# Attention with the last 64 keys of four heads in quarters of the array, two pairs to a turn, and SBUF tiles moved by 32 bytes

## The chip, the cores and the metric

The kernel runs on one core of one Trainium2 chip. The metric is the device time of one execution in microseconds (us). The core has a matrix engine (PE, with its weight loads listed apart as PEld), a vector engine (DVE), a scalar engine (ACT), a general engine (POOL) and a queue engine that issues most DMAs (SP). Operands lie in SBUF, 128 partitions wide; matmul results go to PSUM, which has eight banks of 512 float32 columns per partition.

## What is computed

Three stages follow each other, on 4 batches of 448 tokens, with 12 heads of 64 channels (768 in all):

```python
# 1 attention, per batch and head; q, k, v: (4, 12, 448, 64)
scores = q @ k.T / sqrt(64) - log(448)
x = sigmoid(scores) @ v                      # no softmax: keys can be summed in any order
# 2 gated MLP: w_in 768x1024, w_spatial 448x448, w_out 512x768
h = relu(x @ w_in); u, v = h[..., :512], h[..., 512:]
v_n = (v - mean(v)) / sqrt(var(v) + 1e-6)
v_s = w_spatial @ v_n + b_spatial            # over the tokens of a batch
x = (u * v_s) @ w_out
# 3 MLP with a residual: w_ch1 768x3072, w_ch2 3072x768
xn = (x - mean(x)) / sqrt(var(x) + 1e-6) * g_ln
out = x + relu(xn @ w_ch1) @ w_ch2
```

## The kernel before

**Precision.** Most products are made from operands split in two `float32r` parts, `hi` and `lo`: `mm3` (L258) issues three matmuls, hi x hi (L259), hi x lo (L260) and lo x hi (L261). The product of the attention weights with v is made in plain float32 instead; one such call shows as two rows of PE in the trace, one for each of two passes.

**Memory.** SBUF holds four large tiles that the program cuts up itself: `r_base` and `f_base` for the whole kernel, `r_att` and `f_att` during attention, and after it `r_mlp` and `f_mlp` in their place. The `r_` tiles hold the float32r parts that matmuls read. A tile is placed behind the one before it, rounded up to 32 bytes. `r_base` starts at byte 16,512 of a partition, which is 258 x 64. Behind it the constants (`f_base`, `warm`, the small vectors up to `mhalf`) and the small pool take an odd number of 32-byte steps, so that `r_att`, `f_att`, `r_mlp` and `f_mlp` start 32 bytes past a multiple of 64. All blocks inside a tile are whole multiples of 64 bytes. So an operand is at a multiple of 64 bytes exactly when it lies in `r_base` or `f_base`.

**PSUM.** Two pools: `ps_s` with 2 buffers of two banks (`ps2()`, `wide()`) and `ps_1` with 4 buffers of one bank (`ps1()`). `ps2` takes the scores of a chunk of keys for both heads of a pair, and later the 768 columns of `Project.step` and `ch2`. `ps1` takes the sums of `av`, and the groups of `hv`, `hu`, `spatial`, `ch1` and the transposes of `Project.turn`.

**Attention** (main loop, L755 to L778). The 48 heads are handled as 24 pairs, head `j` of a pair in partitions 64j to 64j+63 of q and k. The host pads k from 448 to 512 keys by repeating the last 64, and the rows of v for the repeated keys are zero. So a pair has four chunks of 128 keys. `qk(p, t)` (L396) does chunks 2t and 2t+1: 6 matmuls of 448 columns each (three products, two heads, each on 64 rows of the array), then one `Sigmoid` on ACT (L410) over 2 x 448 columns. `av(p, t)` (L413) adds up v x weights over the four chunks, head j in columns 64j to 64j+63 of the array (L422). `x_end` (L426) splits a pair's sums into x hi (ACT copy, L288) and x lo (DVE, L289). `qk_split` (L382) makes the parts of q and k for the next pair: casts on DVE (L389, L392), subtractions on POOL (L393, L394) from pair 2 on. The loop runs over half pairs i: `qk(p, 0)`, the split and the loads for later pairs, `av` of the pair before and its `x_end`; then `qk(p, 1)`, and a stretch of background work.

**Background.** `bg` (L743) is a stream of matmul groups of stage 2 for batches 0 to 2: `hv` and `hu`, x times the two halves of w_in, in groups of 18 matmuls. `bg.run(2 * BG_US)` issues some 4.6 us of it, if the x and the weights that it needs are ready (`settled`), else nothing. `jobs.pop` issues weight work: a load on SP, a decode (one ACT op, L277, and three DVE ops, L278 to L282), a split (ACT L288, DVE L289). The four chunks of w_in that `hv` needs come first.

**After attention**: `hv` and `hu` of batch 3, `spatial` (groups of 11 matmuls into `ps1`, each read by one DVE multiply, L558), `Project` (14 steps of 24 matmuls into `wide()`, with `turn`, six transposes, L616, into two `ps1` tiles that ACT and DVE read, L288 and L289), then `mlp`: for each of 12 groups of weights and 4 units of tokens, two groups `ch1` (18 matmuls into `ps1`, read by ACT, L653, then DVE, L654) and the tiles of `ch2` (12 matmuls into `wide()`, read by DVE, L671). In its first group of weights two more `turn`s stand between `ch1` groups (L699). Every engine runs its instructions in program order.

Of the kernel before, what the change touches and what calls it, by code (L numbers as in the profile page):

```python
# [16 lines left out]
P = 128  # L17
B, H, S, D = 4, 12, 448, 64
NPAIR = H // 2
SK = 512  # L20
# [32 lines left out]
PLAIN = range(B * H)  # L53

R_BASE, F_BASE = 23040, 7680
R_ATT, F_ATT = 3840, 9792
# [157 lines left out]
def sigmoid_attention_gmlp_mlp(ctx: ExitStack, tc, q, k, v, w_in, w_sp, w_out, g_ln, w1, w2, out):  # L214
# [4 lines left out]
    ps_s = ctx.enter_context(tc.tile_pool(name="ps_s", bufs=2, space=bass.MemoryType.PSUM))  # L219
    ps_1 = ctx.enter_context(tc.tile_pool(name="ps_1", bufs=4, space=bass.MemoryType.PSUM))  # L220
# [24 lines left out]
    nc.vector.memset(mhalf, -0.5)  # L245

# [100 lines left out]
    k_r = [Ring(R, SK, 2, "att") for _ in range(2)]  # L347
    rv = Ring(F, 512, 3, "att")
    rq = Ring(F, S, 3, "att")
    rk = Ring(F, SK, 3, "att")  # L350
    af_r = Ring(F, 2 * S, 6, "att")
# [13 lines left out]
    @on_pairs  # L365
    def qk_load(p, b, hp):

        qr, kr = rq.next().ap(S), rk.next().ap(SK)
        pairs[p] = dict(raw=(qr, kr))
        for j in range(2):  # L370
            rows = slice(D * j, D * j + D)
            eng = nc.scalar if p < 3 and j else nc.sync
            eng.dma_start(kr[rows], k[b, hp, :, j])
            eng.dma_start(qr[rows], q[b, hp, :D, j])
# [6 lines left out]
    @on_pairs  # L381
    def qk_split(p, b, hp):  # L382
        t = pairs[p]
        qr, kr = t["raw"]
        (qh, ql), (kh, kl) = ([r.next().ap(n) for r in rs] for rs, n in ((q_r, S), (k_r, SK)))
        t.update(qh=qh, ql=ql, kh=kh, kl=kl)
        eng = nc.gpsimd if p > 1 else nc.vector
        if p:
            nc.vector.tensor_copy(kh, kr)  # L389
        else:  # L390
            nc.scalar.copy(kh, kr)
        nc.vector.tensor_copy(qh, qr)  # L392
        eng.tensor_sub(kl, kr, kh)  # L393
        eng.tensor_sub(ql, qr, qh)  # L394

    def qk(p, t):  # L396


        a = pairs[p]
        for c in (2 * t, 2 * t + 1):  # L400
            ps = ps2()
            kc = slice(c * P, (c + 1) * P)
            for i, (w, x) in enumerate((("kh", "qh"), ("kl", "qh"), ("kh", "ql"))):
                for j in range(2):
                    rows = slice(D * j, D * j + D)
                    nc.tensor.matmul(  # L406
                        ps[:, j, :S], a[w][rows, kc], a[x][rows], start=(i == 0), stop=(i == 2)
                    )
            af = af_r.next().ap(2, S)
            nc.scalar.activation(af, ps[:, :, :S], AF.Sigmoid, bias=bias_s, scale=1.0 / math.sqrt(D))  # L410
            a["a", c] = af

    def av(p, t):  # L413

        a = pairs[p]
        if t == 0:
            a["ps"] = ps1()
        for c in (2 * t, 2 * t + 1):
            af = a.pop(("a", c))
            for j in range(2):  # L420
                rows = slice(D * j, D * j + D)
                nc.tensor.matmul(  # L422
                    a["ps"][rows, :S], a["v"][:, 4 * j + c], af[:, j], start=(c == 0), stop=(c == 3)
# [326 lines left out]
    pv_load(0)  # L750
    qk_split(0)
    qk_load(2)
    pv_load(1)
    jobs.pop(1)
    for i in range(2 * n_pairs):  # L755
        p, t = divmod(i, 2)
        now[0] = i
        qk(p, t)
        if t == 0:
            qk_split(p + 1)  # L760
            qk_load(p + 3)
        else:
            pv_load(p + 2)
        if t:
            bg.run(2 * BG_US)
        elif p:
            av(p - 1, 0)
            av(p - 1, 1)
            x_end(p - 1)
        jobs.pop(0 if i < FIRST else 2 if i >= MORE else 1)  # L770
        if i == WO_FROM:
            c0, c1, c2, c3 = wo_chunks
            for job in (c0.load, c1.load, idle, c0.decode, c1.decode, c2.load, c3.load):
                jobs.add([job, idle])
    now[0] += 1
    av(n_pairs - 1, 0)
    av(n_pairs - 1, 1)
    x_end(n_pairs - 1)  # L778
# [172 lines left out]
```

## Time and profile before

| | us |
|---|---|
| median of 3 runs | 1093.79 (1092.7 to 1094.69) |
| the profiled execution | 1092.77 |
| its span, first to last instruction | 1090.8 |
| PE busy, by the page | 1082.0 |
| attention with its background, until | 246.8 |
| `hv`, `hu` of batch 3, and `spatial`, until | 314 |
| `Project`, until | 381 |
| `mlp`, until | 1090.8 |

A row of the timeline is an instruction, or some alike in a row (x12): start, time from the first start to the last end, engine, line, operation, output<-inputs, size, how many; in brackets, idle time of the engine before it and what ended that. Matmuls overlap in the pipeline, so what a matmul costs is read from the distance between starts, not from its length. Row names drop buffer numbers: `r_base,r_mlp` says that one operand lies in the one tile and one in the other. The granted clock (PEclk) is the share of full speed that TensorE had in a stretch.

### The profile page before, as it was taken

Reading aid. Unit: us, or ns where it says so; the run is one execution under the profiler, and the core shown is the slowest. Engines: PE = TensorE matmul, PEld = TensorE weight load, DVE = VectorE, ACT = ScalarE, POOL = GpSimd, SP = SyncE. Lnnn points to the kernel's source line nnn. Section 1 sums busy time; section 2 is a strip of 40 time slices with the busy share of each in tenths; the row PEclk is TensorE's granted clock in tenths of the full one; section 3 lists DMA queues with packets and bytes.
Section 4 is the critical chain, followed back from the end, with each engine's and each line's share of the span. In section 5 each row is a group of like instructions: output and inputs, shape, how many; then the busy total and the mean of one; then the engine's idle time right before and its main releaser. Section 6 shows DMA issues by size and latency. Waiting matters only on the chain.

```text
span 1090.8 us, 14034 instructions
## 1 busy us (share of the span) xinstructions
PE 1082.0 (99%) x5860; PEld 877.3 (80%) x5860; DVE 541.8 (50%) x789; ACT 315.9 (29%) x465; POOL 104.0 (10%) x96
## 2 busy tenths in 40 slices
PE   8999999999999999999999999999999999999998
PEld 5466666668988888888888888888888888888887
DVE  4750113206666856363645555564636364555533
ACT  6754445444533422121112121111212121212110
POOL 1232121202214410000000000000000000000000
PEclk9999999999999999999999999999999999999999
DMA  8743245306610112021111111020202011111013
GB/s 243 220 121 99 94 118 162 122 28 224 208 35 11 48 59 87 29 81 36 59 59 58 59 58 58 29 66 22 88 29 87 30 62 55 58 58 58 1 58 145
DMA packets 31951, 87.94 MB, mean 81 GB/s; under 512 B 7568, under 2 KB 12816, under 8 KB 31760
## 3 DMA queue, kind: packets, MB, share of 16 engines
q1 hardware_dynamic: 29808, 78.97, 22.5%
q0 software_dynamic: 1600, 7.34, 2.0%
q8 instruction: 46, 0.75, 0.3%
q10 hardware_dynamic: 480, 0.74, 0.3%
q14 instruction: 17, 0.14, 0.0%
HBM read 74.17 MB, written 12.86 MB: 80 GB/s over the span
## 4 chain that ended last, share of the span: by engine, by line
PE 99%; ACT 1%; issue 0%; DVE 0%
PE ps L259 28%; PE ps L260 28%; PE ps L261 28%; PE ps L422 7%; PE ps L406 6%; PE ps L616 1%; ACT f_att L410 0%; PE ps L748 0%; PE ps L556 0%; PE ps L555 0%; ACT r_base L288 0%; ACT f_base L277 0%; DVE r_base L289 0%; DVE f_mlp L671 0%; DVE warm L232 0%
## 5 line engine op out<-in xcount | busy, mean ns | idle before, releaser
L671 DVE TENSOR_TENSOR f_mlp<-ps,f_mlp 128x768 f32<-128x768 f32 (+1 forms) x157 | 149.5, 952 | 156.2 <-PE ps L261 156.2
L259 PE MATMUL ps<-r_base,r_mlp 128*128 128x512 f32 (+1 forms) x608 | 216.7, 356 | 0.0
L261 PE MATMUL ps<-r_base,r_mlp 128*128 128x512 f32 (+1 forms) x608 | 216.4, 356 | 0.0
L260 PE MATMUL ps<-r_base,r_mlp 128*128 128x512 f32 (+1 forms) x560 | 197.6, 353 | 0.0
L260 PE MATMUL ps<-r_mlp 128*128 128x512 f32 (+1 forms) x496 | 170.0, 343 | 0.0
L653 ACT ACTIVATE r_mlp<-ps 128x512 fp32r<-128x512 f32 (+1 forms) x96 | 52.1, 543 | 398.5 <-PE ps L261 398.5
L261 PE MATMUL ps<-r_mlp 128*128 128x512 f32 (+1 forms) x460 | 155.2, 337 | 0.0
L259 PE MATMUL ps<-r_mlp 128*128 128x512 f32 x448 | 151.1, 337 | 0.0
L259 PE MATMUL ps<-r_base 128*128 128x512 f32 (+2 forms) x372 | 140.0, 376 | 0.0
L261 PE MATMUL ps<-r_base 128*128 128x512 f32 (+2 forms) x372 | 137.7, 370 | 0.0
L654 DVE SCALAR_TENSOR_TENSOR r_mlp<-ps,r_mlp 128x512 fp32r<-128x512 f32 (+1 forms) x96 | 59.7, 622 | 150.8 <-ACT r_mlp L653 150.8
L261 PEld LDWEIGHTS ps<-r_base,r_mlp 128*128 128x128 f32 x608 | 114.6, 189 | 18.1
L260 PE MATMUL ps<-r_base 128*128 128x512 f32 (+2 forms) x348 | 128.3, 369 | 0.0
L259 PEld LDWEIGHTS ps<-r_base,r_mlp 128*128 128x128 f32 x608 | 114.4, 188 | 17.3
L260 PEld LDWEIGHTS ps<-r_base,r_mlp 128*128 128x128 f32 x560 | 105.3, 188 | 15.0
L260 PEld LDWEIGHTS ps<-r_mlp 128*128 128x128 f32 x496 | 93.4, 188 | 13.0
L410 ACT ACTIVATE f_att<-ps,bias_s 128x896 f32<-128x896 f32 x96 | 91.5, 1005 | 39.3 <-PE ps L406 39.0
L261 PEld LDWEIGHTS ps<-r_mlp 128*128 128x128 f32 x460 | 86.6, 188 | 9.9
L259 PEld LDWEIGHTS ps<-r_mlp 128*128 128x128 f32 x448 | 84.4, 188 | 11.0
L289 DVE TENSOR_TENSOR r_base<-ps,r_base 128x448 fp32r<-128x448 f32 (+1 forms) x48 | 27.3, 586 | 126.8 <-ACT r_base L288 126.8
L259 PEld LDWEIGHTS ps<-r_base 128*128 128x128 f32 x372 | 70.0, 188 | 17.0 <-issue 6.5
L422 PE MATMUL ps<-f_att 128*64 128x448 f32 x384 | 79.1, 555 | 0.0
(90 smaller groups left out, 1216.1 us busy)
## 6 DMA issues: line engine op xcount, KB each, us to landing
f_base<-in_w SPq DMA_DIRECT2D x48, 768.0 KB, 4.2
f_att<-in_v SPq DMA_DIRECT2D x24, 256.0 KB, 2.9
f_base<-in_w_in SPq DMA_DIRECT2D x8, 768.0 KB, 5.3
f_att<-in_k SPq DMA_DIRECT2D x45, 128.0 KB, 3.6
f_att<-in_q SPq DMA_DIRECT2D x45, 112.0 KB, 3.3
out_y<-f_mlp SPq DMA_DIRECT2D x12, 384.0 KB, 2.3
vscr<-f_base SPq DMA_DIRECT2D x14, 256.0 KB, 2.0
uscr<-f_base SPq DMA_DIRECT2D x16, 224.0 KB, 1.9
```

The lines of the kernel that those rows point to most:

```text
L259: nc.tensor.matmul(ps, lh, rh, start=first, stop=False)
L260: nc.tensor.matmul(ps, lh, rl, start=False, stop=False)
L261: nc.tensor.matmul(ps, ll, rh, start=False, stop=last)
L289: eng.tensor_sub(lo, x, hi)
L406: nc.tensor.matmul(ps[:, j, :S], a[w][rows, kc], a[x][rows], start=(i == 0), stop=(i == 2))
L410: nc.scalar.activation(af, ps[:, :, :S], AF.Sigmoid, bias=bias_s, scale=1.0 / math.sqrt(D))
L422: nc.tensor.matmul(a["ps"][rows, :S], a["v"][:, 4 * j + c], af[:, j], start=(c == 0), stop=(c == 3))
L616: nc.tensor.transpose(ps[:, i], xn[:, kc * P : (kc + 1) * P], ident)
L653: nc.scalar.activation(hh[:, f], ps[:, :n], AF.Relu)
L654: nc.vector.scalar_tensor_tensor(hl[:, f], ps[:, :n], 0.0, hh[:, f], op0=ALU.max, op1=ALU.subtract)
L671: nc.vector.tensor_add(y[:, ws], ps, y[:, ws])
```

## The change

- A tile `pad` of 8 float32 (32 bytes) follows `mhalf`, so that the attention tiles and the MLP tiles start at multiples of 64 bytes, as `r_base` does.
- PSUM is cut otherwise: `ps_s` has 3 buffers of two banks, `ps_1` has 2 of one bank. This holds for the whole kernel.
- Attention runs in turns of two pairs. Three chunks of 128 keys are done as before, into three `ps2` tiles. The last 64 keys of the four heads of two pairs are done in one call, `qk_rest`: four plain float32 matmuls on the raw q and k, head j in rows 64j and pair i in columns 64i of the array, then one `Sigmoid`. `av_rest` starts the sums of the two pairs from these, again with four matmuls on 64 rows and 64 columns, into the two banks of one `ps2` tile, and `av` adds the three chunks to it. `sums` does this for the two pairs of the turn before, with both `x_end`s at its end.
- `PLAIN` is empty, so the repeated rows of v are kept (pair i reads rows 64i); k is loaded with 448 columns, not 512. The rings for raw q, k, v and for the weights are deeper.
- In a turn the order is `qk_rest`, `sums`, weight jobs, `qk` of the first pair, a split, loads, weight jobs, background, `qk` of the second pair, a split, loads, weight jobs, background.

```diff
--- before.py
+++ after.py
@@ -17,7 +17,7 @@
 P = 128
 B, H, S, D = 4, 12, 448, 64
 NPAIR = H // 2
-SK = 512
+SM = 3 * P
 DM = H * D
 KC = DM // P
 DFF = 1024
@@ -50,10 +50,11 @@
 VN_DVE = [range(4), range(4), (1, 3), (1, 3)]
 HU_EVERY = 3
 
-PLAIN = range(B * H)
+PLAIN = ()
 
 R_BASE, F_BASE = 23040, 7680
-R_ATT, F_ATT = 3840, 9792
+PAD = 8
+R_ATT, F_ATT = 3328, 12800
 R_MLP, F_MLP = 11904, 9984
 
 PIECE = 1536
@@ -216,8 +217,8 @@
     const = ctx.enter_context(tc.tile_pool(name="const", bufs=1))
     small = ctx.enter_context(tc.tile_pool(name="small", bufs=4))
     dram = ctx.enter_context(tc.tile_pool(name="dram", bufs=1, space=bass.MemoryType.DRAM))
-    ps_s = ctx.enter_context(tc.tile_pool(name="ps_s", bufs=2, space=bass.MemoryType.PSUM))
-    ps_1 = ctx.enter_context(tc.tile_pool(name="ps_1", bufs=4, space=bass.MemoryType.PSUM))
+    ps_s = ctx.enter_context(tc.tile_pool(name="ps_s", bufs=3, space=bass.MemoryType.PSUM))
+    ps_1 = ctx.enter_context(tc.tile_pool(name="ps_1", bufs=2, space=bass.MemoryType.PSUM))
 
     R, F = Arena("r"), Arena("f")
     r_base = const.tile([P, R_BASE], F32R, name="r_base")
@@ -243,6 +244,7 @@
     vnorm = const.tile([P, 2, B, 4], F32, name="vnorm")
     mhalf = const.tile([P, 2, 4], F32, name="mhalf")
     nc.vector.memset(mhalf, -0.5)
+    const.tile([P, PAD], F32, name="pad")
 
     ctx.enter_context(tc.manual_schedule())
 
@@ -344,11 +346,11 @@
     R.add("att", r_att)
     F.add("att", f_att)
     q_r = [Ring(R, S, 2, "att") for _ in range(2)]
-    k_r = [Ring(R, SK, 2, "att") for _ in range(2)]
-    rv = Ring(F, 512, 3, "att")
-    rq = Ring(F, S, 3, "att")
-    rk = Ring(F, SK, 3, "att")
-    af_r = Ring(F, 2 * S, 6, "att")
+    k_r = [Ring(R, SM, 2, "att") for _ in range(2)]
+    rv = Ring(F, 512, 4, "att")
+    rq = Ring(F, S, 4, "att")
+    rk = Ring(F, S, 4, "att")
+    af_r = Ring(F, 2 * S, 8, "att")
     a_rings = [*q_r, *k_r, rv, rq, rk, af_r]
 
     n_pairs = B * NPAIR
@@ -365,12 +367,12 @@
     @on_pairs
     def qk_load(p, b, hp):
 
-        qr, kr = rq.next().ap(S), rk.next().ap(SK)
+        qr, kr = rq.next().ap(S), rk.next().ap(S)
         pairs[p] = dict(raw=(qr, kr))
         for j in range(2):
             rows = slice(D * j, D * j + D)
             eng = nc.scalar if p < 3 and j else nc.sync
-            eng.dma_start(kr[rows], k[b, hp, :, j])
+            eng.dma_start(kr[rows], k[b, hp, :, j, :S])
             eng.dma_start(qr[rows], q[b, hp, :D, j])
 
     @on_pairs
@@ -382,22 +384,28 @@
     def qk_split(p, b, hp):
         t = pairs[p]
         qr, kr = t["raw"]
-        (qh, ql), (kh, kl) = ([r.next().ap(n) for r in rs] for rs, n in ((q_r, S), (k_r, SK)))
+        (qh, ql), (kh, kl) = ([r.next().ap(n) for r in rs] for rs, n in ((q_r, S), (k_r, SM)))
         t.update(qh=qh, ql=ql, kh=kh, kl=kl)
         eng = nc.gpsimd if p > 1 else nc.vector
         if p:
-            nc.vector.tensor_copy(kh, kr)
+            nc.vector.tensor_copy(kh, kr[:, :SM])
         else:
-            nc.scalar.copy(kh, kr)
+            nc.scalar.copy(kh, kr[:, :SM])
         nc.vector.tensor_copy(qh, qr)
-        eng.tensor_sub(kl, kr, kh)
+        eng.tensor_sub(kl, kr[:, :SM], kh)
         eng.tensor_sub(ql, qr, qh)
 
-    def qk(p, t):
+    def sigmoid(ps):
+        af = af_r.next().ap(2, S)
+        nc.scalar.activation(af, ps[:, :, :S], AF.Sigmoid, bias=bias_s, scale=1.0 / math.sqrt(D))
+        return af
+
+    def qk(p):
 
 
         a = pairs[p]
-        for c in (2 * t, 2 * t + 1):
+        a["a"] = []
+        for c in range(3):
             ps = ps2()
             kc = slice(c * P, (c + 1) * P)
             for i, (w, x) in enumerate((("kh", "qh"), ("kl", "qh"), ("kh", "ql"))):
@@ -406,21 +414,39 @@
                     nc.tensor.matmul(
                         ps[:, j, :S], a[w][rows, kc], a[x][rows], start=(i == 0), stop=(i == 2)
                     )
-            af = af_r.next().ap(2, S)
-            nc.scalar.activation(af, ps[:, :, :S], AF.Sigmoid, bias=bias_s, scale=1.0 / math.sqrt(D))
-            a["a", c] = af
-
-    def av(p, t):
+            a["a"].append(sigmoid(ps))
+
+    def qk_rest(p):
+
+
+        ps = ps2()
+        for j in range(2):
+            rows = slice(D * j, D * j + D)
+            for i in range(2):
+                qr, kr = pairs[p + i]["raw"]
+                nc.tensor.matmul(ps[D * i : D * i + D, j, :S], kr[rows, SM:S], qr[rows], start=True, stop=True)
+        pairs[p]["rest"] = sigmoid(ps)
+
+    def av_rest(p):
+
+        ps, af = ps2(), pairs[p].pop("rest")
+        for i in range(2):
+            rows = slice(D * i, D * i + D)
+            a = pairs[p + i]
+            a["ps"] = ps[:, i]
+            for j in range(2):
+                nc.tensor.matmul(
+                    a["ps"][D * j : D * j + D, :S], a["v"][rows, 4 * j + 3], af[rows, j], start=True, stop=False
+                )
+
+    def av(p):
 
         a = pairs[p]
-        if t == 0:
-            a["ps"] = ps1()
-        for c in (2 * t, 2 * t + 1):
-            af = a.pop(("a", c))
+        for c, af in enumerate(a.pop("a")):
             for j in range(2):
                 rows = slice(D * j, D * j + D)
                 nc.tensor.matmul(
-                    a["ps"][rows, :S], a["v"][:, 4 * j + c], af[:, j], start=(c == 0), stop=(c == 3)
+                    a["ps"][rows, :S], a["v"][:, 4 * j + c], af[:, j], start=False, stop=(c == 2)
                 )
 
     def x_end(p):
@@ -747,35 +773,51 @@
     for _ in range(WARM):
         nc.tensor.matmul(ps1()[:, :P], warm, warm, start=True, stop=True)
     qk_load(1)
-    pv_load(0)
     qk_split(0)
     qk_load(2)
+    qk_load(3)
+    pv_load(0)
     pv_load(1)
-    jobs.pop(1)
-    for i in range(2 * n_pairs):
-        p, t = divmod(i, 2)
+
+    def weights(i):
         now[0] = i
-        qk(p, t)
-        if t == 0:
-            qk_split(p + 1)
-            qk_load(p + 3)
-        else:
-            pv_load(p + 2)
-        if t:
-            bg.run(2 * BG_US)
-        elif p:
-            av(p - 1, 0)
-            av(p - 1, 1)
-            x_end(p - 1)
         jobs.pop(0 if i < FIRST else 2 if i >= MORE else 1)
         if i == WO_FROM:
             c0, c1, c2, c3 = wo_chunks
             for job in (c0.load, c1.load, idle, c0.decode, c1.decode, c2.load, c3.load):
                 jobs.add([job, idle])
+
+    def sums(p):
+        av_rest(p)
+        av(p)
+        av(p + 1)
+        x_end(p)
+        x_end(p + 1)
+
+    jobs.pop(1)
+    for p in range(0, n_pairs, 2):
+        if p:
+            qk_rest(p)
+            sums(p - 2)
+            weights(2 * p)
+        qk(p)
+        qk_split(p + 1)
+        if not p:
+            qk_rest(p)
+        else:
+            pv_load(p)
+            pv_load(p + 1)
+        weights(2 * p + 1)
+        bg.run(2 * BG_US)
+        qk(p + 1)
+        qk_split(p + 2)
+        qk_load(p + 4)
+        qk_load(p + 5)
+        weights(2 * p + 2)
+        weights(2 * p + 3)
+        bg.run(2 * BG_US)
     now[0] += 1
-    av(n_pairs - 1, 0)
-    av(n_pairs - 1, 1)
-    x_end(n_pairs - 1)
+    sums(n_pairs - 2)
     now[0] = 10**9
     for r in a_rings:
         r.free()
```

## Rows read from the trace of the kernel before

**Rows 1.** The page's part 4: share of the chain that ended last, by engine.

```profile
PE 99%; ACT 1%; issue 0%; DVE 0%
```

**Rows 2.** Busy time by stage (windows), with columns in the first line.

```profile
core 0: us, PE busy (x) PEld busy (x) DVE busy (x) ACT busy (x) POOL busy (x), PEclk, DMA share, GB/s
27.10:32.00 4.90, 4.90 (x20) 1.54 (x18) 3.20 (x6) 2.69 (x3) 0.88 (x1) 0.65 0.98 272
55.40:246.80 191.40, 191.40 (x1091) 125.88 (x1089) 42.88 (x85) 92.70 (x116) 42.98 (x34) 1.00 0.35 106
```

**Rows 3.** Timeline of PE, 106 to 113 us: one pair, columns as told above.

```profile
106.28 0.39 PE L261 MATMUL ps<-r_base 128*128 128x512 f32 x1
106.59 1.48 PE L406 MATMUL ps<-r_att 64*128 64x448 f32 x12
108.01 3.23 PE L422 MATMUL ps<-f_att 128*64 128x448 f32 x16
111.17 1.49 PE L406 MATMUL ps<-r_att 64*128 64x448 f32 x12
112.58 0.50 PE L259 MATMUL ps<-r_base 128*128 128x512 f32 x1
112.91 0.39 PE L260 MATMUL ps<-r_base 128*128 128x512 f32 x1
```

**Rows 4.** Timeline of PE: first and last of 15 matmuls of 448 columns.

```profile
102.08 0.37 PE L259 MATMUL ps<-r_base 128*128 128x448 f32 x1
...
104.92 0.36 PE L261 MATMUL ps<-r_base 128*128 128x448 f32 x1
```

**Rows 5.** Timeline of PE, 25 to 32 us: a stop and what follows it.

```profile
25.43 1.77 PE L406 MATMUL ps<-r_att 64*128 64x448 f32 x12 [1.64 <-ACT f_att L410]
27.13 4.90 PE L422 MATMUL ps<-f_att 128*64 128x448 f32 x16
```

**Rows 6.** The page's part 5: the sigmoids.

```profile
L410 ACT ACTIVATE f_att<-ps,bias_s 128x896 f32<-128x896 f32 x96 | 91.5, 1005 | 39.3 <-PE ps L406 39.0
```

**Rows 7.** Timelines of DVE and POOL, 28 to 33 us: decode, casts, subtraction.

```profile
28.75 0.96 DVE L279 SCALAR_TENSOR_TENSOR f_base<-f_base 128x768 uint32<-128x768 uint32 x1
...
30.62 0.42 DVE L389 CAST r_att<-f_att 128x512 fp32r<-128x512 f32 x1
...
31.12 1.35 POOL L393 TENSOR_TENSOR r_att<-f_att,r_att 128x512 fp32r<-128x512 f32 x1 [9.20 <-DVE r_att L389]
```

**Rows 8.** Groups by line and shape: two of six of 512 columns reading `r_mlp`.

```profile
L259 PE MATMUL ps<-r_base,r_mlp 128*128 128x512 f32 x400 | 158.4, 396 | 0.0
...
L260 PE MATMUL ps<-r_mlp 128*128 128x512 f32 x272 | 107.0, 393 | 0.0
```

**Rows 9.** Timeline of PE: first and last of two `ch1` groups of 18.

```profile
437.22 0.39 PE L259 MATMUL ps<-r_base 128*128 128x512 f32 x1
...
441.08 0.39 PE L261 MATMUL ps<-r_base 128*128 128x512 f32 x1
441.31 0.39 PE L259 MATMUL ps<-r_base,r_mlp 128*128 128x512 f32 x1
...
445.29 0.40 PE L261 MATMUL ps<-r_base,r_mlp 128*128 128x512 f32 x1
```

**Rows 10.** Timelines of DVE and PE in `spatial`, 291 to 296 us.

```profile
294.65 1.15 DVE L558 TENSOR_TENSOR f_base<-ps,f_mlp 128x448 f32<-128x448 f32 x2
...
291.45 0.36 PE L259 MATMUL ps<-r_mlp,r_base 128*128 128x448 f32 x1
```

**Rows 11.** Timelines of PE and DVE, 380 to 392 us: transposes, then `ch1`.

```profile
381.14 0.48 PE L259 MATMUL ps<-r_base,r_mlp 128*128 128x512 f32 x1
...
383.42 0.55 DVE L289 TENSOR_TENSOR r_base<-ps,r_base 128x384 fp32r<-128x384 f32 x1
...
389.66 0.82 PE L616 MATMUL ps<-warm,f_base 128*128 128x128 f32 x6
...
390.49 0.69 DVE L654 SCALAR_TENSOR_TENSOR r_mlp<-ps,r_mlp 128x512 fp32r<-128x512 f32 x1 [2.42 <-ACT r_mlp L653]
```

## The prediction

> **What bounds the kernel now.** I read the page's chain first: it is 99% PE [rows 1], so time is gained only where PE gets less to do or waits less, and anything that makes PE wait is lost at once. The busy time by stage says the same of attention: PE is busy for all of 55 to 247 us, ACT for under half of it [rows 2]. The timeline of one pair then shows what PE pays per piece: 12 matmuls of `qk` take 1.42 us, 16 rows of `av` take 3.16 us, twelve of `qk` again, then background [rows 3]. Before 55 us it is otherwise: there is little background, and PE stops for the sigmoids, 1.64 us at 25.43; after that stop the mean granted clock is 0.65 and `av` takes 4.90 us where it takes 3.23 later [rows 2, 3, 5]. Last come two `ch1` groups side by side: the same moving x, the weights once in `r_base` and once in `r_mlp`, and different distances between starts [rows 9]. They price the 32 bytes.
>
> **Part 1, fewer matmul slots in attention.** Distance of two full 448-column matmuls: (104.92 - 102.08) / 14 = 0.203 us [rows 4]. In `qk` the two heads use different rows of the array and run side by side, so 12 matmuls are 6 slots, 1.22 us; the other 0.20 of the 1.42 is the change of array shape at both ends. `av`: I take 0.15 of the 3.16 as such change, which leaves 3.01 for 8 calls, 0.376 a call, or 0.75 for the two heads together. At the border to background there is 0.31 instead of 0.23 before `qk`, and 0.33 after it [rows 3, 9], some 0.19 per stretch.
>
> Two pairs before: 4 x 1.42 + 2 x 3.16 + 2 x 0.19 = 12.4 us. After: `qk` of three chunks is 9 slots, 1.83 + 0.20, twice: 4.05. `av` of three chunks: 6 calls, twice, 4.51, and 0.10 to leave it. The background borders stay at 0.38. `qk_rest` and `av_rest` are four calls each on a quarter of the array. A call on half of it costs 0.376; if four quarters fit as two halves do, a quarter call costs half, and a group 0.75. With about 0.3 for entering and leaving them: 1.8. Sum 10.85, saved 1.55 a turn. The trace has no quarter, so the bounds: a call at its half-array share, two at a time, 1.50 a group; each alone, 3.0 a group (four times 0.75). Below 0.75 I exclude, for the products are the same plain float32 ones. I take 0.75, because side by side in rows is what the `qk` slots show and in columns what `av`'s share fits, and rows and banks are dealt out as there.
>
> The Trainium skill has a rule against this: "TensorE: Matmul & The Clock Gate", Part 3, "The mechanism", says that matmuls start and end strictly in program order. The program lists both passes of a quarter before the next quarter, so by that rule a group would be five pass slots, over twice mine. No row here settles it; it is a rival below, priced from `av`.
>
> **The first three turns** gain less. There ACT paces PE: 8 sigmoids of 1.005 us per two pairs [rows 6], against 12.4 us of PE, beside decodes and splits. After, 7. Three turns save 3 sigmoids, 3 us, and 3 x 1.55 on PE, not both. Against this stands a new queue: in a turn `weights(2p)` now comes ahead of `qk_split(p + 1)` on DVE; before, the split came first. A decode's two long ops (0.96 each), its short one, a weight split, the casts (0.42) and POOL's 1.35 [rows 7] make some 7 us after `sums`, while `qk(p)` gives PE 2 us of cover. With background behind `qk(p)` the 4.6 us more hide most of it; without, in turns 2 and 4, PE stands some 2 to 5 us, as it stood 1.64 us at 25.43, perhaps with the half clock again. The third `ps2` buffer takes away stops like that one, which waited for a sigmoid to free a buffer. I take +3 us of gain for these turns, from -4 to +6. Loads: `pv_load` and `qk_load` move by a turn on SP, behind weight loads, but come two turns ahead through rings of four. Attention: 9 x 1.55 + 3 = **17.0 us saved**, 10 to 20 with quarters at 0.75.
>
> **Part 2, the 32 bytes.** In the group that reads only `r_base` the distance is (441.08 - 437.22) / 17 = 0.227 us; in the next, with weights in `r_mlp`, (445.29 - 441.31) / 17 = 0.234 [rows 9]. 7 ns each. Of 512-column matmuls, 400 + 400 + 352 mix `r_base` and `r_mlp` [rows 8], another 192 in `Project` the other way round: 1,344 x 7 ns = 9.4 us. Where both operands are in `r_mlp` (272 + 224 + 224 = 720) both are off by the same 32 bytes; I take half, 3.5 ns: 2.5 us, between 0 and 5. The some 130 of 448 columns with one operand in `r_mlp` give under 1 us at 7 ns; I leave them out, as those of 256 columns. Not every aligned group need be as even as that one, so I take **10.5 us saved** out of 11.9, bounds 6 and 14.
>
> Beside this stands the Trainium skill's "SBUF — State Buffer", Specifications (TRN2): cachelines of 16 bytes. By that a shift of 32 bytes changes nothing and the sum would be 10.5 us worse. The two groups disagree with it here: 0.227 against 0.234.
>
> **Part 3, two `ps1` instead of four.** This costs at two places, by whether a tile is read before its buffer is asked for again two tiles later. In `spatial`, DVE lags: the fifth group's multiply, the first of the two in the DVE row, ends near 295.27, while PE starts the seventh group at 291.45 [rows 10]. With four buffers that is hidden; with two the seventh waits 3.8 us. The lag is DVE's own backlog, so PE waits once by its greatest size, and what it has waited stays: **4 us lost** (0 to 6). Where `Project` hands over to `mlp`, six transposes fill both `ps1`, and the first `ch1` starts at 381.14, while DVE reads the first at 383.42 to 383.97 [rows 11]: 2.8 us. Two more `turn`s follow between `ch1` groups: the second half of each waits for the `ch1` group just finished, read by ACT and then DVE until 391.18, 1.2 us after PE asks for it at some 389.95, and the next `ch1` a little more: 1.4 each. Together **5.6 us lost** (3 to 7). In `mlp` proper two `ch1` groups alternate with over 8 us of `ch2`, which covers 1.2 us: nothing. In attention `av` no longer uses `ps1`, and a background group takes over 4 us: nothing. The third `ps2` gains nothing later, since no wait for one is left there.
>
> **Sum.** -17.0 - 10.5 + 4 + 5.6 = -17.9 us on the profiled execution's 1092.77 gives 1074.9. The median is 1.0 above that execution: **1076 us**.
>
> **The rivals.**
> 1. *Two `ps1` cost more, or the early turns do* (DVE's queue, half clock in turns 0 to 4). For it: the stop and the slow `av` of [rows 5]; against: one buffer more for scores. It adds 8 to 14 us: 1084 to 1090. Chance 0.15.
> 2. *Quarters two at a time*, the program-order rule, 1.50 a group: 24 groups x 0.75 = 18 us more, 1094, no change. For it: the two passes of a call are neighbours in the program. Against: `av` has the same two passes and still gets 0.376 a call, half of what 0.75 would be alone. Chance 0.13.
> 3. *Slower: the quarters take turns*, each alone, 3.0 a group: 24 x 2.25 = 54 us more, 1130. It would be in `qk_rest` and `av_rest` alone. It decides from 1.5 us a group: there the whole gain of 18 us is gone. Against: rows overlap in `qk`. Chance 0.05.
> 4. *The 32 bytes do nothing* (the change doesn't do what it says): 0.234 stays, 10.5 us less gain, 1086. Against: [rows 9]. Chance 0.07.
>
> **How the numbers follow.** Forecast 0.60, spread by its bounds (attention 10 to 20, 32 bytes 6 to 14, buffers 3 to 13) over 1065 to 1087; rivals as above. Left out at 1094 and over: rival 3 and half of rival 2, and at the low end a little: range 1064 to 1094. A measurement of this kernel can tell 0.2%, 2.2 us, from no change. Faster than 1091.6: 0.60 + 0.07 + nearly all of rival 1 + a third of rival 2, 0.85. Same: 0.06, rival 2. Slower: 0.09, rivals 2 and 3.
>
> **What would show it.** `L406` with 18 rows in 2.0 us, `av` of two pairs with 24 rows in some 4.6 us, and between them two groups of float32 rows on 64 rows and 64 columns, 0.75 us each: right; 1.5 or 3.0: rivals 2 or 3. `ch1` starts 0.227 apart in every group: part 2 right; 0.234: rival 4. PE idle or late by some 4 us in `spatial`, released by DVE L558, and 2.8, 1.4 and 1.4 us at the first `ch1` groups, released by L289: part 3 right. Attention's end should come near 230 us. A long PE gap released by POOL L394 or DVE L389 in turns 2 and 4 shows the queue. The forecast is wrong if any one of the quarter price, the 7 ns or the buffer waits is off by its factor.

## The result and the profile after

The changed kernel takes 1107.56 us (median; 1106.9 to 1108.84), the kernel before 1093.8 beside it: a ratio of 1.0132, 95% interval 1.0119 to 1.0144. It is 1.3% slower where 1076 us, 1.6% faster, was forecast; the time lies above the range. The profiled execution's span is 1105.1 us against 1090.8.

The page of the changed kernel: span, PE's busy time, and its part 4, the chain that ended last, by engine, which answers to [rows 1].

```profile
span 1105.1 us, 13989 instructions
PE 1071.6 (97%) x5812; PEld 870.3 (79%) x5812; DVE 544.6 (49%) x789; ACT 304.6 (28%) x453; POOL 98.1 (9%) x96
PE 88%; issue 4%; DMA 3%; DVE 3%; ACT 1%; POOL 1%; SPq 0%; POOLq 0%; ACTq 0%
```

PE held 99% of the chain before, it holds 88% now: PE does less and waits more. Where, the busy time by stage tells, with the columns of [rows 2]. First the kernel before, in four stretches: attention up to 62 us, attention up to the last `av`, the stretch up to the first `ch1`, the mlp.

```profile
5.62:62.00 56.38, 52.25 (x303) 28.15 (x303) 37.34 (x55) 40.62 (x50) 15.83 (x12) 0.97 0.81 225
62.00:246.84 184.84, 184.84 (x1056) 120.51 (x1054) 37.32 (x77) 88.14 (x110) 39.76 (x32) 1.00 0.34 106
246.84:381.14 134.30, 134.30 (x730) 119.65 (x729) 94.56 (x195) 59.27 (x110) 43.75 (x45) 1.00 0.32 105
381.14:1090.00 708.86, 706.08 (x3759) 604.62 (x3757) 371.79 (x459) 125.77 (x194) 4.49 (x3) 1.00 0.17 57
```

The same four stretches of the kernel after:

```profile
5.73:62.00 56.27, 44.33 (x265) 22.96 (x266) 33.16 (x49) 33.90 (x41) 11.55 (x10) 0.90 0.70 215
62.00:251.89 189.89, 180.38 (x1046) 117.65 (x1043) 43.00 (x82) 82.85 (x105) 38.13 (x34) 0.99 0.32 102
251.89:392.98 141.09, 135.73 (x730) 119.36 (x728) 98.18 (x203) 61.96 (x114) 45.48 (x46) 1.00 0.30 103
392.98:1105.00 712.02, 706.50 (x3756) 605.92 (x3756) 369.49 (x452) 123.86 (x190) 2.76 (x3) 1.00 0.16 57
```

Attention ends 5.1 us later and began 0.1 later, the middle is 6.8 us longer, and the rest, from the first `ch1` to the span's end, takes 712.1 us for 709.7: 4.9 + 6.8 + 2.4 = 14.1 of the 14.3 us that the spans differ by. In attention PE's busy time fell from 237.1 to 224.7 us: 12.4 us of work are gone, as meant, although more of it ran at half clock (the mean clock up to 62 us is 0.90 for 0.97). But its idle time rose from 4.1 to 21.4. The waits of PE name the releasers (columns: who waited for whom, us in all, times, longest):

```profile
PE ps L414 <- DVE r_base L291: 14.7, 11, 2.7
PE ps L414 <- DVE r_att L394: 4.3, 1, 4.3
PE ps L261 <- DVE r_base L291: 2.6, 1, 2.6
PE ps L642 <- DVE r_mlp L680: 2.2, 2, 1.1
```

`L414` is `qk`. The first row was in no part of the forecast. The chain from 100 to 108 us, one turn (start, duration, what; pieces of "issue" left out), shows what it is:

```profile
99.88 4.68 PE ps L448 x24
...
104.59 0.54 ACT r_base L290
...
105.15 0.64 DVE r_base L291
...
105.81 0.54 ACT r_base L290
...
106.38 0.64 DVE r_base L291
...
107.15 0.87 PE ps L414 x6
```

After the 24 rows of `av` (`L448`) come the two splits of `x_end`, one pair after the other: copy, subtraction, copy, subtraction. The second copy reads the other bank of the PSUM tile, and still it starts only when the first subtraction is done. All four read the one `ps2` tile that both pairs' sums now share, and `qk`'s third chunk is the third `ps2` asked for since. Two chunks of scores, 12 rows from 104.47 on, are all the cover there is: PE stands from about 105.97 to 107.15, 1.18 us. The same gap of 1.18 or 1.19 us stands in each of the eight later turns. The Trainium skill, "Perfetto Trace Analysis", Optimization Strategy, reads a gap that repeats on the engine that should be full as a possible sign of too little SBUF or PSUM for the next tile; the trace agrees, with 1.18 us in eight turns, although the change had added a third `ps2`.

The early turns, rows of DVE and PE from 23 to 28 us; the stop in the last answers to that of [rows 5]:

```profile
23.88 0.96 DVE L284 SCALAR_TENSOR_TENSOR f_base<-f_base 128x768 uint32<-128x768 uint32 x1
24.75 0.95 DVE L291 TENSOR_TENSOR r_base<-f_base,r_base 128x768 fp32r<-128x768 f32 x1
...
25.89 0.39 DVE L394 CAST r_att<-f_att 128x448 fp32r<-128x448 f32 x1
...
26.42 1.50 PE L414 MATMUL ps<-r_att 64*128 64x448 f32 x4 [4.26 <-DVE r_att L394]
```

The casts for the next pair now stand on DVE behind a weight decode and a weight split, as the prediction said they would; PE waits 4.26 us for them, and from 23.84 us on the granted clock is 0.5 for 10.24 us, of which PE works in 7.27. At the handover to the mlp, the row that answers to the first of [rows 11]:

```profile
392.98 0.80 PE L261 MATMUL ps<-r_base,r_mlp 128*128 128x512 f32 x1 [2.63 <-DVE r_base L291]
```

The 2.63 us are the 2.8 forecast; two waits of 1.08 us at the next transposes (`L642`, fourth of the waits above) follow. Here too the clock fell, from 392.48 to 395.89 us; PE works in 2.91 us of that, so half clock cost some 1.5, an estimate.

The forecast's price for the quarters is in the timeline of PE, 98 to 105 us:

```profile
98.15 0.98 PE L427 MATMUL ps<-f_att 64*64 64x448 f32 x8
98.95 0.93 PE L438 MATMUL ps<-f_att 64*64 64x448 f32 x8
99.81 4.73 PE L448 MATMUL ps<-f_att 128*64 128x448 f32 x24
104.47 1.50 PE L414 MATMUL ps<-r_att 64*128 64x448 f32 x12
```

From start to start `qk_rest` takes 0.80 us and `av_rest` 0.86, 1.66 together where 1.8 was forecast; `av` takes 4.66 for 4.61. The stretch from 98.1 to 98.5 us alone holds the first pass of each of the four quarters of `qk_rest`:

```profile
98.15 0.61 PE L427 MATMUL ps<-f_att 64*64 64x448 f32 x4
```

All four are done 0.61 us after the first start, and each takes 0.59: the quarters run side by side.

### The profile page after: what moved, and what is told of

Read it like the earlier page. It is cut to its first block, busy times and chain, and to the rows that moved or that the text cites. A ratio compares the mean times of both kernels' runs of the same rounds, so it can differ in the third digit from the quotient of the medians.

```text
span 1105.1 us, 13989 instructions
## 1 busy us (share of the span) xinstructions
PE 1071.6 (97%) x5812; PEld 870.3 (79%) x5812; DVE 544.6 (49%) x789; ACT 304.6 (28%) x453; POOL 98.1 (9%) x96
## 3 DMA queue, kind: packets, MB, share of 16 engines
q1 hardware_dynamic: 29808, 78.23, 21.4%
## 4 chain that ended last, share of the span: by engine, by line
PE 88%; issue 4%; DMA 3%; DVE 3%; ACT 1%; POOL 1%; SPq 0%; POOLq 0%; ACTq 0%
PE ps L261 27%; PE ps L263 26%; PE ps L262 26%; PE ps L448 4%; PE ps L414 3%; DMA f_base<-in_w_in 1%; DVE r_base L291 1%; ACT r_base L290 1%; DMA f_att<-in_k 1%; PE ps L427 1%; PE ps L642 1%; PE ps L438 1%; DMA f_mlp<-in_w_sp 0%; DVE f_base L281 0%; DVE f_base L284 0%
## 5 line engine op out<-in xcount | busy, mean ns | idle before, releaser
L400 ACT ACTIVATE f_att<-ps,bias_s 128x896 f32<-128x896 f32 x84 | 79.9, 1009 | 34.3 <-PE ps L427 17.2
L261 PEld LDWEIGHTS ps<-r_base 128*128 128x128 f32 x372 | 70.3, 189 | 18.1 <-issue 6.1
L263 PEld LDWEIGHTS ps<-r_base 128*128 128x128 f32 x372 | 70.4, 189 | 11.0
```

The costliest lines, as they stand in the source:

```text
L261: nc.tensor.matmul(ps, lh, rh, start=first, stop=False)
L263: nc.tensor.matmul(ps, ll, rh, start=False, stop=last)
```

## The experiments

The theory after the traces: the matmul work is saved as forecast, and given back by (a) the splits that hold a `ps2` tile in every turn, (b) DVE's order in the early turns, (c) two single PSUM tiles, as forecast; and (d) the 32 bytes are worth little. Each got a run of its own; then all together. Ratios are to the kernel before on the same chip, where the change itself stands at 1.0132. Differences in us are between medians that were partly taken on different chips, on which the kernel before took 1092.9 to 1093.8 us; a us between two runs on different chips shows little.

**The 32 bytes alone**, in the kernel before:

```diff
     nc.vector.memset(mhalf, -0.5)
+    const.tile([P, 8], F32, name="pad")
```

> The kernel before with the 32 unused bytes alone; attention and the cut of the PSUM stay as before. Theory A (the prediction's part 2): the 7 ns between matmuls of 512 columns whose moving operand starts at 32 bytes past a multiple of 64 go, and 3.5 ns for those that start there in part; 1344 x 7 + 720 x 3.5 ns = 11.9 us less, of which 10.5 us on the path, so about 1083 us. Theory B (read from the trace of the changed kernel, where the mean distance of matmuls of 512 columns in the mlp fell only from 232.0 to 230.9 ns): the distance is not set by the 64 bytes; 2136 matmuls x 1.1 ns = 2.4 us less at most, so 1091 to 1094 us.

1091.7 us, ratio 0.9983 (0.9975 to 0.9992): 1.3 us less by the medians, not 10.5. The groups by line and shape (busy us, mean ns) of the large group that answers to [rows 8], and one that reads `r_base` alone:

```profile
L260 PE MATMUL ps<-r_base,r_mlp 128*128 128x512 f32 x400 | 157.9, 395 | 0.0
...
L262 PE MATMUL ps<-r_base 128*128 128x512 f32 x228 | 89.1, 391 | 0.0
```

396 ns became 395. Theory B holds.

**96 bytes in place of 32** (`[P, 24]` for `[P, 8]`):

> The kernel before with 96 unused bytes in place of 32: every operand of the mlp again starts at a multiple of 64, but 64 bytes further on. Theory A (only the multiple of 64 counts): the same time as with 32 bytes, to within 1.5 us, and 1083 us if the prediction's part 2 holds. Theory B (the distance between matmuls is set by where a tile lies, but not by the multiple of 64): a time that differs from that with 32 bytes by more than 1.5 us, either way, with the distance of matmuls of 512 columns on the tile of the mlp weights (232 to 234 ns in both kernels so far) changed.

1092.01 us, ratio 0.9990 (0.9981 to 0.9999). It is within 0.3 us of the run before, so the second half of theory A, that one multiple of 64 is as good as another, is not contradicted; its 1083 us is.

**The 32 bytes ahead of all tiles**, which moves every tile of the arenas by 32 bytes and leaves their distances from each other as they were:

```diff
+    const.tile([P, 8], F32, name="pad")
     r_base = const.tile([P, R_BASE], F32R, name="r_base")
```

> The kernel before with the 32 unused bytes put ahead of all other tiles, so that the tile r_base, and with it the operands of its matmuls, now starts 32 bytes past a multiple of 64, while the mlp's weights in r_mlp start at one. Theory A (the distance of 227 or 234 ns is set by the multiple of 64): the matmuls of 512 columns on r_base alone (median 227 ns so far in every kernel) rise by up to 7 ns; with some 660 of them in the stages ahead of the mlp and the first chunk's share in it 4 to 9 us more than with the bytes behind r_base, 1096 to 1101 us. Theory B (the multiple of 64 is worth 1 to 2 ns at most, and what tells 227 from 233 ns is that one operand lies in r_base and the other in r_mlp): the median on r_base alone stays at 227 ns and the time within 1.5 us of that with the bytes behind r_base, 1090 to 1093 us.

1093.19 us, ratio 0.9996 (0.9987 to 1.0005): no difference from the kernel before. Theory A's 1096 to 1101 us are out; against the run with the bytes behind `r_base` it is 1.5 us, at the edge of what theory B allowed. The groups by line and shape, and the timeline of the two `ch1` groups of [rows 9]:

```profile
L260 PE MATMUL ps<-r_base,r_mlp 128*128 128x512 f32 x400 | 158.4, 396 | 0.0
...
L262 PE MATMUL ps<-r_base 128*128 128x512 f32 x228 | 89.0, 390 | 0.0
...
437.27 0.39 PE L260 MATMUL ps<-r_base 128*128 128x512 f32 x1
...
441.13 0.39 PE L262 MATMUL ps<-r_base 128*128 128x512 f32 x1
441.36 0.39 PE L260 MATMUL ps<-r_base,r_mlp 128*128 128x512 f32 x1
...
445.34 0.40 PE L262 MATMUL ps<-r_base,r_mlp 128*128 128x512 f32 x1
```

With `r_base` now 32 bytes past a multiple of 64 (by the program's layout; a trace shows no addresses) its group still has (441.13 - 437.27) / 17 = 0.227 us; with `r_mlp` at a multiple the other still has (445.34 - 441.36) / 17 = 0.234. Both are the values of [rows 9], with the alignments exchanged. The multiple of 64 is not what tells the two groups apart.

**PSUM cut back to two double and four single tiles after attention**, in the changed kernel:

```diff
-    ps_s = ctx.enter_context(tc.tile_pool(name="ps_s", bufs=3, space=bass.MemoryType.PSUM))
-    ps_1 = ctx.enter_context(tc.tile_pool(name="ps_1", bufs=2, space=bass.MemoryType.PSUM))
+    pools = {}
+
+    def cut(stack, two, one):
+        for key, n in (("s", two), ("1", one)):
+            pools[key] = stack.enter_context(tc.tile_pool(name=f"ps_{key}{n}", bufs=n, space=bass.MemoryType.PSUM))
+
+    ps_att = ExitStack()
+    cut(ps_att, 3, 2)
...
     bg.run(1e9)
+    ps_att.close()
+    cut(ctx, 2, 4)
```

> The changed kernel, with the PSUM cut back to two double and four single tiles once the attention and its background are done; attention itself keeps three double and two single. Theory (the prediction's part 3, and the trace of the changed kernel): the gaps of PE behind the spatial sums (.49, 1.17, .35, .73 us) and at the handover to the mlp (2.63, 1.085 twice) with the 3.4 us at half clock behind them go: 9 to 10.4 us less than the changed kernel, so about 1097 to 1099 us. Rival: the handover waits for the normalization itself and not for a tile, and the PE gaps come again elsewhere: within 2 us of 1107.6 us.

1099.18 us, ratio 1.0060 (1.0046 to 1.0074): 8.4 us less than the changed kernel. The gaps in `spatial` and at the handover are gone from the waits; these two stay or are new:

```profile
PE ps L420 <- DVE r_base L297: 14.9, 11, 2.7
PE ps L267 <- DVE r_base L297: 2.6, 1, 2.6
```

The first is (a), untouched (the lines are 6 further down here). The second, at 253.5 us, comes with the cut itself: the first matmul behind it waits for the last split of attention, and 3.4 us at half clock follow. So the two single tiles had cost more than 8.4 us; a later run shows how much.

**A third stretch of background work in a turn**, between the sums and the next scores:

```diff
             weights(2 * p)
+            bg.run(4 / 3 * BG_US)
...
-        bg.run(2 * BG_US)
+        bg.run(4 / 3 * BG_US)
...
-        bg.run(2 * BG_US)
+        bg.run(4 / 3 * BG_US)
```

> The changed kernel with three stretches of background work in a turn in place of two, each 4/3 of the length, so that one lies between the sums of a turn and the first scores of the next. Theory (the splits of the sums hold the PSUM tile that the scores' third chunk wants, 11 waits with 14.7 us in all): these waits go to under 2 us; against it stands some .39 us a turn for one more change between the two kinds of work, so 9 to 12 us less than the changed kernel, 1096 to 1099 us. Rival (the wait only moves, since the sigmoids or the next split then come last): 0 to 4 us less, 1104 to 1108 us.

1097.38 us, ratio 1.0036 (1.0024 to 1.0048): 10.2 us less. The row of (a) in PE's waits is down from 14.7 us in 11 waits to

```profile
PE ps L414 <- DVE r_base L291: 1.3, 1, 1.3
```

A turn with 48 background matmuls of 448 columns (the last such turn, from the first row of `av` of one turn to that of the next) took 22.10 us before as two pairs (216.21 to 238.31), 22.13 in the changed kernel (207.43 to 229.56), and 20.90 here (201.34 to 222.24). The wait had eaten the whole gain of a turn.

**One split for both pairs' sums**: one copy and one subtraction of 896 columns.

```diff
         x_end(p)
-        x_end(p + 1)
...
-        xh, xl = (t[:, hp] for t in x_of(b))
-        split(xh, xl, pairs.pop(p)["ps"][:, :S])
+        xh, xl = (t[:, hp : hp + 2] for t in x_of(b))
+        split(xh, xl, pairs.pop(p)["both"][:, :, :S])
...
```

> The changed kernel with the sums of both pairs of a turn split by one ACT copy and one DVE subtraction of twice the size, in place of two of each in the order copy, subtraction, copy, subtraction. Theory (the four run one after the other because they read one PSUM tile, .53 + .62 + .53 + .62 us and the ways between): the chain is shorter by two handovers and two fixed costs, some .5 to .6 us of the 1.18 us that PE waits in each of 11 turns: 5 to 7 us less, 1101 to 1103 us. Rival (the order is not forced by the tile, ACT or DVE being late for other reasons): 0 to 2 us less.

1100.6 us, ratio 1.0061 (1.0049 to 1.0073): 7.0 us less. The gap of a later turn is 0.71 us for 1.18, the row of (a)

```profile
PE ps L414 <- DVE r_base L291: 10.0, 11, 1.8
```

4.7 us of the 7.0 are this row; some more lies in the early turns, where the 4.26 us gap is 3.10 here and the half clock behind it lasts 6.8 us in place of 10.24. It confirms that the length of the chain sets the gap; that the tile forces its order was not tried by itself.

**The next pair's casts first**, ahead of the sums and of the weight decode:

```diff
             qk_rest(p)
+            qk_split(p + 1)
             sums(p - 2)
...
         qk(p)
-        qk_split(p + 1)
         if not p:
+            qk_split(p + 1)
             qk_rest(p)
```

> The changed kernel with the cast and split of the next pair's q and k issued ahead of the sums and of the weight decode, in place of behind them. Theory (in the early turns PE waits for casts that stand behind the decode on DVE: gaps of 4.26, 1.33 and about .7 us, and 10.2 us at half clock behind them): the gaps and most of the half clock go, 6 to 10 us less, 1098 to 1102 us. Rival (the loads or ACT pace these turns, or the splits of the sums, now behind the casts, make the wait at the scores' third chunk longer): 2 us less to 4 us more, 1105 to 1112 us.

1104.46 us, ratio 1.0101 (1.0088 to 1.0114): 3.1 us less, between the two expectations. The gap of 4.26 us is gone; the largest left near it is 0.80, a wait for a sigmoid. But two others grew; the waits, and one of them in the timeline:

```profile
PE ps L414 <- DVE r_base L291: 15.9, 11, 3.2
...
35.16 0.95 DVE L291 TENSOR_TENSOR r_base<-f_base,r_base 128x768 fp32r<-128x768 f32 x1
36.02 0.35 DVE L391 CAST r_att<-f_att 128x384 fp32r<-128x384 f32 x1
36.29 0.39 DVE L394 CAST r_att<-f_att 128x448 fp32r<-128x448 f32 x1
...
36.59 0.62 DVE L291 TENSOR_TENSOR r_base<-ps,r_base 128x448 fp32r<-128x448 f32 x1
...
38.58 1.49 PE L414 MATMUL ps<-r_att 64*128 64x448 f32 x6 [2.00 <-DVE r_base L291]
```

Now the sums' subtraction stands behind a weight split and the casts, and cause (a) grows by 1.2 us, a part of what (b) loses: one queue, two users. Half clock remains from 24.81 for 3.4 us, from 38.46 for 3.4 and from 55.53 for 6.8.

**The four edits together:**

> The changed kernel with all four edits: PSUM cut back after attention, three stretches of background work in a turn, the next pair's split first, and one split for both pairs' sums. Theory (the four causes are separate): the gains add up except that the shorter split chain is worth little once work lies above it: 10 + 10 + 8 us less than 1107.6, about 1079 to 1083 us, below the kernel before. Rival (the causes share the early turns, and the later turns become bound by DVE): 1088 to 1095 us, no better than the kernel before.

1085.55 us, ratio 0.9929 (0.9916 to 0.9942): 22.0 us less than the changed kernel and 0.7% below the kernel before. One by one the edits gave 8.4 + 10.2 + 7.0 + 3.1 = 28.7; two of them act on the same wait. The theory's 1079 to 1083 is missed by 2.6 us, of which the gap that the cut brings is the plainest part. Two runs went after that and after the early turns.

**Two single tiles passed over behind the cut:**

```diff
     cut(ctx, 2, 4)
+    for _ in range(2):
+        ps1()
```

> All four edits together, and two single tiles passed over behind the cut, so that the first matmuls behind it use the two banks that were single before and not the one that the last sums are still read from. Theory: the gap of 2.1 us at the end of attention (PE waiting for the subtraction of the last split) and the 3.4 us at half clock behind it, worth 1.7, go: 3.8 us less than with the four edits, about 1081.7 us. Rival (that gap is the wait for the last x itself): the same time, 1085.5 us.

1084.57 us, ratio 0.9918 (0.9901 to 0.9934), its executions from 1081.81 to 1088.25, so no difference from the four edits that this spread could show. The gap stayed:

```profile
242.09 0.50 PE L267 MATMUL ps<-r_base 128*128 128x512 f32 x1 [2.13 <-DVE r_base L297]
```

So which of the new pool's tiles the first matmul uses does not decide it. That left the rival, the last x, or the closing of the pools as such. In this run's profile the clock did not fall behind the gap.

**And the second weight job of the three early turns behind the next sums:**

```diff
+    EARLY = 6
...
+            if p <= EARLY:
+                weights(2 * p - 1)
             weights(2 * p)
...
-        weights(2 * p + 3)
+        if p + 2 > EARLY:
+            weights(2 * p + 3)
```

> As the run before, and in the three early turns the second weight job of a turn issued behind the sums of the next, so that the split of the sums no longer stands behind a decode of 2.5 us on DVE. Theory (what is left of the early stage's loss is DVE's order): the gaps of 2.38 us at 22.55 and of 1.5 to 1.9 us at 38 to 55 shrink, 2 to 4 us less, 1078 to 1080 us. Rival (the first background work waits for exactly these weights): nothing to 3 us more, 1082 to 1085 us.

1082.13 us, ratio 0.9901 (0.9888 to 0.9913): 2.4 us less than the run before, within what the theory said of the step (its 1078 to 1080 had counted on 1081.7 to start from). The intervals of the two runs overlap, so the times alone do not settle this step; the traces speak for it. In the run before, gaps of 1.97 and 1.74 us stood at 53.5 and 56.0, with 6.8 us at half clock. Here no gap above 1.1 us is left ahead of attention's end, and up to there the granted clock stays at 1.0.

**Only the third double tile given back**, in place of closing both pools:

```diff
+    ps_att = ExitStack()
+    ps_x = ps_att.enter_context(tc.tile_pool(name="ps_x", bufs=1, space=bass.MemoryType.PSUM))
+    twos, ones = [ps_s, ps_s, ps_x], [ps_1, ps_1]
...
     ps_att.close()
-    cut(ctx, 2, 4)
-    for _ in range(2):
-        ps1()
+    ps_y = ctx.enter_context(tc.tile_pool(name="ps_y", bufs=2, space=bass.MemoryType.PSUM))
+    twos[:] = [ps_s]
+    ones += [ps_y, ps_y]
+    turns["one"] = 0
```

`ps2` and `ps1` take from the pools in these lists in turn.

> As the run with the later weight jobs, but in place of closing both PSUM pools only the third double tile, in a pool of its own, is given back after attention and cut in two singles; the first matmuls behind it take the two singles that were there all along. Theory (the 2.13 us gap at the end of attention is a new pool waiting for all of the old one, since passing over two tiles left it where it was): the gap and the half clock behind it go, 3.8 us less than 1082.1, about 1078 to 1079 us. Rival (it is the wait for the last x, which the shorter attention now shows): the same time, 1081 to 1083 us.

1078.58 us (1078.15 to 1079.65), ratio 0.9863 (0.9846 to 0.9879), 3.6 us less than the run before. The page (span, PE, the granted clock by slices) and the longest waits of PE:

```profile
span 1077.8 us, 13943 instructions
PE 1064.6 (99%) x5812; PEld 866.4 (80%) x5812; DVE 540.2 (50%) x777; ACT 301.5 (28%) x441; POOL 97.6 (9%) x96
...
PEclk9999999999999999999999999999999999999999
...
PE ps L269 <- ACT r_base L298: 2.0, 2, 1.0
PE ps L435 <- ACT f_att L408: 1.7, 2, 0.9
```

The gap at attention's end is gone; `hv` follows `av` at once:

```profile
235.53 0.55 PE L457 MATMUL ps<-f_att 128*64 128x448 f32 x2
236.01 0.50 PE L269 MATMUL ps<-r_base 128*128 128x512 f32 x1
```

So the gap came from closing the pools, not from x. By stage, this kernel has attention 10.8 us shorter than the kernel before, the middle 0.4 and the mlp 1.7, by the starts of the last row of `av`, the first `ch1` and the last matmul. In its chain one `qk` of 18 rows takes 2.02 us, the forecast's 2.0.

## Why the prediction was wrong

**The views and PE as the bound: right.** All that PE waits for is lost at once; that is why 17 us of new idle time show in full.

**Part 1, the prices: right.** Quarters at 0.75 a group with 0.3 for the change of shape: 1.66 for 1.8. `av` and `qk` within 0.05 us. Without the wait a turn is 1.2 us shorter although it has one stretch of background more, which was priced at 0.19: 1.4, for the 1.55 forecast.

**Part 1, the wait: the step that failed.** "The third `ps2` gains nothing later, since no wait for one is left there." The change made one: it puts both pairs' sums in one double tile and calls `x_end` twice straight ahead of `qk`, whose third chunk takes that tile. The prediction counted PE slots and the sigmoids' buffers, but not who reads the sums, for how long, and what PE has to do until then: 2.4 us of split (104.59 to 107.01) against 1.4 us of scores (to 105.97). Every piece stood in the code and the diff; before, the two pairs' splits lay apart. That the wait is for the splits is shown by two runs; that it is the shared tile which keeps the second copy behind the first subtraction is read from the code, and no run separates it. Price 14.7 us of PE waits; the third stretch of background alone gave back 10.2.

**Part 1, the early turns: mechanism right, size and sign wrong.** The queue (decode ahead of the casts on DVE), the stop of "2 to 5 us" (4.26) and the half clock were all named, and then +3 us of gain was taken, "from -4 to +6". With other stops of 1.33 and 2.65 us and 13.7 us at half clock, the changed kernel needs 64.0 us from the first `av` to that of the fourth turn; the last experiment does the same in 54.9. The kernel before takes 52.0 us for the same six pairs, with 18 background matmuls fewer, some 4.1 us: about 8 us lost, where 3 were taken as gained. Ends that far apart were to be decided by the nearest row, and that was [rows 5], a stop with half clock behind it.

**Part 2: wrong attribution.** [Rows 9] show two groups that differ in the tile, in its alignment, and in whether both operands lie in one tile. The 7 ns were put down to the alignment, with nothing to separate the three. The runs moved the alignment alone: 0.227 and 0.234 stayed, and 10.5 us were 1.3. In attributing 7 ns to alignment it set aside the rule of the Trainium skill, "SBUF — State Buffer", Specifications (TRN2), that cachelines have 16 bytes; by that rule a shift by 32 bytes changes nothing, and moving all tiles by 32 bytes changed nothing (a ratio of 0.9996).

**Part 3: right in its sum and at the handover, in `spatial` partly by luck.** Forecast 4 + 5.6 = 9.6 us. Giving the tiles back shortened the middle and the mlp by 141.6 - 134.4 = 7.2 and 708.4 - 704.1 = 4.3 us (changed kernel against the last experiment, by the same starts): 11.4, with the half clock at the handover, some 1.5, among them. Ahead of the handover, where [rows 10] stand, PE's gaps were 0.49, 1.17, 0.35 and 0.73 us, and the rest is lateness below the gaps read here. Only the last two gaps, 1.1 us, wait for the multiply of `spatial` that the forecast named; the first two wait for ACT (L509, L538), which reads the groups of `hv` and `hu` and was priced at nothing.

**The sum.** Attention was forecast 17.0 shorter and came 4.9 longer: 21.9 us. The 32 bytes: 9.2. PSUM: 1.8. Together 32.9, for a miss of 31.6. Of the 21.9 some 11 lie in the early turns, with 5.2 of the new wait's 14.7 us among them, and 9.5 are the eight later waits.

**The rivals.** 1 came in part: the early turns and the half clock, but priced at 8 to 14 us where this and the unseen wait of every turn came together. 4 came. 2 and 3, the quarters, fell: 0.80 and 0.86 are neither 1.5 nor 3.0. The rule weighed there, the Trainium skill's "TensorE: Matmul & The Clock Gate", Part 3, "The mechanism", that matmuls start and end in program order, was read as one quarter waiting for another; the trace shows four side by side (0.61 us for their first passes), which the rule as it stands need not exclude, if a call with its two passes counts as one matmul. What happened was in no rival: a wait put in place of nothing, by a tile two readers share.

**The range** did not hold 1107.6. It was built from bounds of named terms; the unnamed one was as large as the whole forecast gain.

## What to carry to other kernels

When two results are put in one PSUM tile, list its readers in order, add their times, and set the sum against what PE can do until it asks for that tile again; two short splits one after the other outlast two chunks of scores. When an order is changed, ask of each engine's queue what now stands ahead of the piece PE waits for, and try filler between producer and next user: here it gave back 10.2 us of a loss of 13.8, without touching the matmuls. Before a difference of a few ns is multiplied by a thousand, find two groups that differ in one property only.

## What the runs showed of the hardware

- Moving every tile by 32 bytes left the matmuls' times as they were (158.4 us in 400 of them in both kernels); moving `r_mlp` alone by 32 bytes took 0.5 us from these, by 96 bytes nothing (158.5). So what counts is how far the two tiles lie apart, if anything does. What makes 0.227 of one group and 0.233 of the other is open; it wasn't tried to move the weights of one group into the other tile.
- The granted clock of PE fell to 0.5 behind stops of 4.26, 2.65 and 2.63 us, for 10.24, 3.41 and 3.41 us, and not behind the eight stops of 1.18 us. In the kernel before it fell at 27.13 us, behind the stop of 1.64 us, for 3.41; with the casts first it fell at 24.81 us, behind stops of 1.18 and 0.80 us in a row, for 3.41. Behind 2.13 us at the end of attention it fell in two of three profiles (of the four edits together and of the later weight jobs, not of the two tiles passed over). In the last experiment no stop is longer than 1.1 us and the clock stays at 1.0 to the end of the mlp. What half clock costs beside the stop is half of the time that PE works in it: an estimate of 3.6 us of the 10.24, and of 1.5 to 1.7 of a stretch of 3.41. In the kernel before, `av` took 4.90 us in place of 3.23 over such a stretch, 1.67 more.
- Four products of 64 rows by 64 columns of float32, two passes each, take 0.80 and 0.86 us a group of four, start to start; the first passes of all four are done within 0.61 us.
- Closing the PSUM pools and opening new ones made the first matmul behind wait 2.1 to 2.6 us for the last reader of the old, also with two of the new tiles passed over; giving back one tile and going on in the others cost nothing that the trace shows.
